# Attention, Fourier mixing and feed-forward: the second layer's weights later, their bits in PSUM, and rests and folds on GpSimd

## The chip, the core and the metric

One core of one Trainium2 chip. The time is device microseconds from start to end of one execution; three runs of the kernel before gave 1315.07 to 1316.8 us, median 1316.18. The profile is of one more execution. Times in it count from its first instruction. In the profile PE is TensorE (PEld its weight loads), DVE is VectorE, ACT is ScalarE, POOL is GpSimd and SP is SyncE, which here only issues DMAs; SPq and ACTq are DMA-issuing instructions of an engine.

## The reference

```
scores = q @ k.T / sqrt(64)               # q, k, v: 8 batches x 8 heads x 576 x 64
mask by blocks of 64: block_i >= block_j;  attn = softmax(scores);  o = attn @ v
x = o as [8, 576, 512]
u = x + real(fft(fft(x, axis=1), axis=2))
un = (u - mean(u)) / sqrt(var(u) + 1e-6)
out = u + relu(un @ w_ch1) @ w_ch2        # 512 -> 2048 -> 512
```

## The kernel before

The 64 heads go one after the other, eight to each of the eight batches `b`. Everything is written out without loops on the chip. Float32 accuracy is kept by splitting operands in a leading part and a rest.

*A head h.* `load_head` brings q and k (`raw`, two buffers). `lead` (ACT, L293) rounds them into `LEAD`; `rest(h, 0)` (DVE, L308) and `rest(h, 1)` (POOL, L310) subtract to get the rests; `lead_copies` are two DMAs within the chip that stack rests and leads (L301, L302). `max_part` 0 to 3 multiply q by k for the row maxima, which DVE reduces (L388, L392, L394) into `M`; `shift` transposes them on PE, ACT negates (L403) and a small DMA puts them in a row of `LEAD` (L405). `scores` 0 to 3 multiply again with the shift in; ACT makes two exponentials of each piece (`ph` in f16 at L434, `p32` in f32 at L435), POOL subtracts for the low half `pl` (L436). `values` multiply `ph` and `pl` by `VH` and `VL`; DVE divides (L471 to L474), and every second head its pair goes to DRAM (`xd`).

*A batch b.* When its eight heads are through, `mirror` loads the rows back, half of them by indirect DMAs from POOL. `folded` (L549, L550) makes sums (name "c") and differences (name "s") of rows and columns, `split32` splits them, `stage1`, `stage1_tail`, `stage2_sin` and `stage2_cos` are the transforms on PE, and `stage2_cos` ends with sums into `X` and `U` (L633, L634; on DVE for b = 0, on POOL otherwise). `normalized_steps` normalises 256 rows at a time and hands them to a *feed*: `first` (16 columns f of the first layer, four parts each, into `h`, then ACT and DVE make `gh` and `gl`, L749 and L750) and `second` (two for each f, into `acc`). There are 18 feeds; first and second layer alternate by pairs of f.

*The weights.* `w_ch1` and `w_ch2` come as 64-bit numbers. They land in 14 loads of 1 MB (two rows of tiles, "double") and 4 of 0.5 MB (L826, SP's queue), at most three ahead. For each landing `weight_single` makes float32 bits by three DVE operations (L836, L837, L838) in `W`, and ACT squares them (L839) for a scale. Landings 0 to 7 are the first layer, the rest the second. `weight_scale` makes a layer's scale; `weight_parts` cuts a tile into two f16 parts (ACT L863, L866 and POOL L867 for the first layer; ACT L863 and DVE L869 for the second). One lane of such steps holds both layers in turn.

*The order.* PE's instructions keep the order in which a planner in the kernel's source writes them down. It has lanes of `Step`s (heads, maxima, scores, values, transform), each with a cost on PE, a chain of costs on other engines ("D0.9" is 0.9 us of DVE, "A", "G", "Q", "L" are ACT, POOL, SP's queue and plain latency), what it comes after, and a `place` for priority. It picks the step that is ready and has the smallest place, fills gaps with feed steps (`filler`), and puts weight steps (`side`) in where their first engine's queue is short (`AHEAD`). Steps of later batches wait for all weights ("w32"). PSUM has eight banks: one `av`, three `ps`, two `h`, two `acc`; until the first feed all of the last seven are lent to the heads (`lent`). Other engines' instructions, and DMA issues in each queue, follow in the order of the scheduler of the tile framework, in order on each engine.

Of the kernel before, what the change touches and what calls it, by code (L numbers as in the profile page):

```python
# [20 lines left out]
DM = H * D  # L21
# [31 lines left out]
def _d(width):  # L53
    return f"D{0.19 + 0.00102 * width}"

# [123 lines left out]
def tile_attn_fourier_ffn(  # L179
# [7 lines left out]
    ps = {name: pool(name, n, space=PSUM) for name, n in BANKS.items()}  # L187
# [60 lines left out]
    queues = {x: Queue() for x in "DAGQ"}  # L248
# [3 lines left out]
    lent = list(BANKS)  # L252
# [4 lines left out]
    def ready(step):  # L257
        r = max((done[x] for x in step.after), default=0.0)
        return max(r, min(rings[x][0] for x in lent)) if step.bank else r

    def issue(step):
# [7 lines left out]
        for engine, cost in step.chain:  # L269
            if engine == "B":  # L270
                free = t + HOP
            else:
                t = t + cost if engine == "L" else queues[engine].book(t + HOP, cost)
# [21 lines left out]
    def quick(h):  # L295

        return nc.scalar if h < H else nc.sync

    def lead_copies(h):
        x0, x1 = REST[h % NB].bitcast(F32), LEAD[h % NB].bitcast(F32)  # L300
        quick(h).dma_start(x0[D:P, 0:S], x1[0:D, 64:64 + S])  # L301
        quick(h).dma_start(x0[0:D, S:], x1[0:D, 64 + S:])  # L302

    def rest(h, which):

        x0, x1, raw = REST[h % NB], LEAD[h % NB].bitcast(F32), raws[h]
        if which == 0:
            nc.vector.tensor_tensor(x0[0:D, 0:S], raw[:, 0:S], x1[0:D, 64:64 + S], op=ALU.subtract)  # L308
# [40 lines left out]
    def prepare_lane():  # L349
        for h in range(B * H):  # L350
# [4 lines left out]
            yield Step(lambda: lead_copies(h), 0.0, ("A1.0" if h < H else "Q1.2", "L2.2"), (("T", h),), ("TC", h), place=h - 0.9)  # L355
            yield Step(lambda: rest(h, 0), 0.0, (_d(S),), (("T", h),), ("T2", h, 0), place=h - 0.8)
            yield Step(lambda: rest(h, 1), 0.0, (_g(S),), (("T", h),), ("T2", h, 1), place=h - 0.8)

    def v_lane():
        for g in range(B * H // 2):  # L360
# [6 lines left out]
                lambda: split_v(g), 0.11, ("D0.46", "B", "A0.83", "D0.88"), (("NS", g),), ("N", g), True,  # L367
# [3 lines left out]
    def max_part(h, n):  # L371
# [21 lines left out]
        if n == 3:  # L393
            nc.vector.tensor_tensor(m[:, 4:5], m[:, 4:5], m[:, 5:6], op=ALU.max)  # L394
# [3 lines left out]
    def shift(h):  # L398
# [6 lines left out]
        quick(h).dma_start(dst.bitcast(F32), mt.bitcast(F32))  # L405
# [88 lines left out]
    def max_lane():  # L494
        for h in range(B * H):
# [5 lines left out]
            yield Step(lambda: shift(h), 0.12, ("A0.26", "B", "A0.5" if h < H else "Q0.6", "L2.2"), (("M", h),), ("X", h), True, place=h - 0.6)  # L501
# [20 lines left out]
    def fourier_steps(b):  # L522
# [23 lines left out]
        def folded(op, width, name, c):  # L546
            r = (128, 128, 33)[c]
            e = work.tile([P, DM], F32, name="tmp", bufs=2)
            nc.vector.tensor_tensor(e[0:r], X[c][0:r], U[c][0:r], op=op)  # L549
            nc.vector.tensor_tensor(e[0:r, 1:256], e[0:r, 1:256], e[0:r, 511:256:-1], op=op)  # L550
# [65 lines left out]
        def stage2_cos(c):  # L616
# [14 lines left out]
            engine = nc.vector if b == 0 else nc.gpsimd  # L631
# [13 lines left out]
            mirror, 0.0, ("G3", "L2.5"), (("V", H * b + H - 1, 4),), D_("u"),  # L645
# [367 lines left out]
```

## Time and profile before

| | |
|---|---|
| median of three runs | 1316.18 us |
| profiled execution | 1315.5 us, span 1313.7 us |
| mean granted TensorE clock | 0.951 |
| busy: PE, DVE, ACT, POOL | 1184.2, 671.9, 548.5, 530.0 us |
| DMA moved | 99.10 MB |

A row of groups has the line, the engine, the operation, what it writes and reads with shapes and count; then busy time, mean nanoseconds of one, and the idle time of the engine before them with what ended it. A row of a time line has start, length, engine, line, operation, and in brackets idle time before it. A row of waits has the waiting engine and line, the one waited for, the sum in microseconds, how often, and the longest.

### The profile page before, as it was taken

The numbers are of one execution on the slowest core, as the hardware profiler recorded it, in microseconds if no ns is written. First come the engines' busy times: TensorE is split into PE (matmuls) and PEld (weight loads), VectorE is DVE, ScalarE is ACT, GpSimd is POOL, SyncE is SP. The second block draws the span as 40 slices with busy tenths as digits, with TensorE's granted clock in tenths as the row PEclk, the third lists the DMA queues.
The fourth block names the chain that finished last, engine by engine and source line by source line (L and its number), as shares of the span: only waits on it lengthen the run. The fifth ranks groups of instructions, "written<-read, shape, count | busy, mean of one in ns | idle before, by whom it ended". The sixth has DMA issues, their size and how long they took to land.

```text
span 1313.7 us, 25264 instructions
## 1 busy us (share of the span) xinstructions
PE 1184.2 (90%) x10068; PEld 886.7 (67%) x10068; DVE 671.9 (51%) x1440; ACT 548.5 (42%) x1137; POOL 530.0 (40%) x578
## 2 busy tenths in 40 slices
PE   3464469999898999999999999999899999999998
PEld 2363357777676777677777777777677767767665
DVE  6983776445645564655546544746372432412211
ACT  3569355545354444444545354544543112111110
POOL 4668143444544553455443645436442500300000
PEclk9955679999699999999999999999999999999999
DMA  9756213232223223322242133223211000000000
GB/s 280 230 175 177 93 29 77 84 106 64 61 65 92 76 50 90 93 76 51 80 115 75 44 96 104 73 70 86 79 30 49 30 12 17 22 1 17 16 17 17
DMA packets 55941, 99.10 MB, mean 75 GB/s; under 512 B 7709, under 2 KB 26605, under 8 KB 55696
## 3 DMA queue, kind: packets, MB, share of 16 engines
q1 hardware_dynamic: 52176, 87.56, 23.5%
q0 software_dynamic: 2288, 7.54, 1.9%
q10 hardware_dynamic: 1360, 2.38, 0.6%
q8 instruction: 80, 1.31, 0.4%
q14 instruction: 37, 0.30, 0.1%
HBM read 58.46 MB, written 18.87 MB: 59 GB/s over the span
## 4 chain that ended last, share of the span: by engine, by line
PE 76%; DVE 10%; ACT 4%; DMA 3%; POOL 3%; issue 3%; SPq 0%; ACTq 0%; DVEq 0%; POOLq 0%
PE h L194 27%; PE acc L194 26%; PE ps L194 16%; PE av L194 5%; POOL pl L436 2%; PE ps L197 1%; DVE M L392 1%; DVE W L837 1%; DMA W<-in_moe_w_ch_dram 1%; DVE rest L308 1%; DVE W L838 1%; ACT lead L293 1%; DVE tmp L549 1%; DMA U<-xd,rows 1%; DVE W L836 1%
## 5 line engine op out<-in xcount | busy, mean ns | idle before, releaser
L194 PE MATMUL h<-uh,W 128*128 128x256 f16 x2304 | 434.9, 275 | 0.0
L436 POOL TENSOR_TENSOR pl<-p,ph 128x288 f16<-128x288 f32 (+1 forms) x256 | 257.9, 1017 | 395.8 <-ACT p L435 249.6
L194 PEld LDWEIGHTS <-W 128*128 128x128 f16 x3456 | 325.8, 99 | 64.3 <-issue 4.0
L194 PE MATMUL acc<-W,gh 128*128 128x512 f16 x1152 | 347.2, 383 | 0.0
L194 PE MATMUL h<-ul,W 128*128 128x256 f16 x1152 | 316.2, 274 | 0.0
L194 PE MATMUL acc<-W,gl 128*128 128x512 f16 x576 | 220.1, 382 | 0.4 <-DVE gl L750 0.4
L750 DVE SCALAR_TENSOR_TENSOR gl<-h,gh 128x512 f16<-128x512 f32 x144 | 98.9, 687 | 227.3 <-ACT gh L749 227.2
L194 PE MATMUL ps<-lead 72*128 72x64 f32 (+9 forms) x700 | 196.5, 342 | 12.5 <-ACT lead L293 6.8
L749 ACT ACTIVATE gh<-h 128x512 f16<-128x512 f32 x144 | 85.9, 596 | 268.4 <-PE h L194 267.7
L434 ACT ACTIVATE ph<-ps 128x512 f16<-128x512 f32 (+1 forms) x229 | 116.0, 507 | 121.0 <-PE ps L194 119.7
L194 PEld LDWEIGHTS <-gh 128*128 128x128 f16 x1152 | 101.0, 99 | 87.8 <-issue 8.2
L392 DVE TENSOR_REDUCE M<-ps 128x1 f32<-128x320 f32 (+3 forms) x235 | 120.5, 527 | 47.9 <-PE ps L194 46.7
L194 PE MATMUL av<-VH,pl 128*128 128x65 f16 x960 | 115.9, 200 | 31.7 <-POOL pl L436 31.5
L194 PEld LDWEIGHTS ps<-lead 72*128 72x128 f32 (+1 forms) x700 | 125.6, 201 | 20.8 <-ACT lead L293 6.8
L194 PEld LDWEIGHTS <-ph 128*128 128x128 f16 x1920 | 113.0, 103 | 34.1 <-DVE x L474 8.4
L310 POOL TENSOR_TENSOR rest<-raw,lead 64x576 fp32r<-64x576 f32 x64 | 116.2, 1816 | 23.3 <-ACT lead L293 18.5
L194 PE MATMUL av<-VH,ph 128*128 128x65 f16 x960 | 118.1, 202 | 8.2 <-DVE x L474 7.6
L194 PE MATMUL ps<-rest 128*128 128x64 f32 (+2 forms) x345 | 121.6, 360 | 1.8 <-DVE M L392 1.1
L435 ACT ACTIVATE p<-ps 128x512 f32<-128x512 f32 (+1 forms) x229 | 115.9, 506 | 10.2 <-POOL pl L436 10.1
L194 PE MATMUL av<-VL,ph 128*128 128x64 f16 x960 | 117.3, 200 | 0.0
L194 PEld LDWEIGHTS <-pl 128*128 128x128 f16 x960 | 93.6, 102 | 34.9 <-POOL pl L436 34.8
L308 DVE TENSOR_TENSOR rest<-raw,lead 64x576 fp32r<-64x576 f32 x64 | 60.0, 938 | 88.4 <-ACT lead L293 88.3
(171 smaller groups left out, 1376.7 us busy)
## 6 DMA issues: line engine op xcount, KB each, us to landing
raw<-in_qk_dram SPq DMA_DIRECT2D x64, 288.0 KB
rest<-lead SPq DMA_DIRECT2D x112, 144.0 KB
W<-in_moe_w_ch_dram SPq DMA_DIRECT2D x14, 1024.0 KB
V<-in_v_dram SPq DMA_DIRECT2D x32, 320.0 KB
xd<-x SPq DMA_DIRECT2D x32, 256.0 KB
out_dram<-u SPq DMA_DIRECT2D x32, 256.0 KB
u<-xd SPq DMA_DIRECT2D x8, 512.0 KB
dft<-in_c_dft_dram POOLq DMA_DIRECT2D x1, 2606.0 KB, 11.3
```

The costliest lines, as they stand in the source:

```text
L194: return tc.keep_in_program_order(nc.tensor.matmul(*args, **kw))
L197: return tc.keep_in_program_order(nc.tensor.transpose(*args, **kw))
L293: nc.scalar.copy(LEAD[h % NB][0:D, 64:], raws[h])
L308: nc.vector.tensor_tensor(x0[0:D, 0:S], raw[:, 0:S], x1[0:D, 64:64 + S], op=ALU.subtract)
L310: nc.gpsimd.tensor_tensor(x0[D:P, S:], raw[:, S:], x1[0:D, 64 + S:], op=ALU.subtract)
L392: nc.vector.tensor_reduce(m[:, j:j + 1], t[:, at - hi:at], axis=AX.X, op=ALU.max)
L434: nc.scalar.activation(ph[:, at:at + w], t[:, 0:w], AF.Exp, scale=0.125)
L435: nc.scalar.activation(p32[:, 0:w], t[:, 0:w], AF.Exp, scale=0.125)
L436: nc.gpsimd.tensor_tensor(pl[:, at:at + w], p32[:, 0:w], ph[:, at:at + w], op=ALU.subtract)
L549: nc.vector.tensor_tensor(e[0:r], X[c][0:r], U[c][0:r], op=op)
L749: nc.scalar.activation(gh, t, AF.Relu)
L750: nc.vector.scalar_tensor_tensor(gl, t, 0.0, gh, op0=ALU.max, op1=ALU.subtract)
```

## The change

- The first two of the three bit operations write into a PSUM tile (`bits`, the two banks of `acc`) instead of `W`.
- `acc` becomes one tile of two banks instead of two tiles of one, and is no longer lent to the heads: five banks are lent instead of seven.
- Weight loads are issued by ACT's queue; copies of the leads and shifts of heads 0 to 7 by SP's.
- There are two weight lanes, one for each layer. The second layer's landings are worked on only after the first layer's scale and the scores of head 5. Heads of later batches wait for the folds of batch 0 instead of for all weights.
- The first feed does all its first layer before its second; its `gh` and `gl` from column 4 on lie in buffers of the transform.
- `rest(h, 0)` of heads 0 to 15, the differences among the folds of batch 0 and its sums into `X` and `U` go from DVE to POOL.
- The last step of the row maxima is a `tensor_scalar` instead of a `tensor_tensor`.
[...]

```diff
-    ps = {name: pool(name, n, space=PSUM) for name, n in BANKS.items()}
+    ps = {name: pool(name, 1 if name == "acc" else n, space=PSUM) for name, n in BANKS.items()}
...
-    queues = {x: Queue() for x in "DAGQ"}
+    queues = {x: Queue() for x in "DAGQK"}
...
-    lent = list(BANKS)
+    lent = ["ps", "h"]
...
+    def book(engine, t, cost):
+        used = [queues[x] for x in {"X": "DK", "G": "GK", "P": "G"}.get(engine, engine)]
+        while True:
+            at = max(x.fit(t, cost) for x in used)
+            if at <= t:
+                return max(x.book(t, cost) for x in used)
+            t = at
...
-        quick(h).dma_start(x0[D:P, 0:S], x1[0:D, 64:64 + S])
-        quick(h).dma_start(x0[0:D, S:], x1[0:D, 64 + S:])
+        nc.sync.dma_start(x0[D:P, 0:S], x1[0:D, 64:64 + S])
+        nc.sync.dma_start(x0[0:D, S:], x1[0:D, 64 + S:])
...
-            nc.vector.tensor_tensor(x0[0:D, 0:S], raw[:, 0:S], x1[0:D, 64:64 + S], op=ALU.subtract)
+            engine = nc.gpsimd if h < 16 else nc.vector
+            engine.tensor_tensor(x0[0:D, 0:S], raw[:, 0:S], x1[0:D, 64:64 + S], op=ALU.subtract)
...
-            nc.vector.tensor_tensor(m[:, 4:5], m[:, 4:5], m[:, 5:6], op=ALU.max)
+            nc.vector.tensor_scalar(m[:, 4:5], m[:, 4:5], m[:, 5:6], None, op0=ALU.max)
...
-        quick(h).dma_start(dst.bitcast(F32), mt.bitcast(F32))
+        nc.sync.dma_start(dst.bitcast(F32), mt.bitcast(F32))
...
+            engine = nc.gpsimd if b == 0 and name == "s" else nc.vector
+            engine.tensor_tensor(e[0:r], X[c][0:r], U[c][0:r], op=op)
+            engine.tensor_tensor(e[0:r, 1:256], e[0:r, 1:256], e[0:r, 511:256:-1], op=op)
...
-            engine = nc.vector if b == 0 else nc.gpsimd
+            engine = nc.gpsimd
...
+    KEEP = [(f"z{x}{m}", [P, 2, n], 1) for x, n in (("c", NCOS), ("s", NSIN)) for m in range(2)]
+    KEEP += [(f"fs{m}", [P, 2, KCOL], 1) for m in range(2)]
...
+            if me == 1 and f > 3:
+                name, shape, bufs = KEEP[f // 2 - 2]
+                both = work.tile(shape, F32R, name=name, bufs=bufs).rearrange("p x n -> p (x n)").bitcast(F16)
+                gh, gl = both[:, 0:4 * P], both[:, 4 * P:8 * P]
...
-            if f == 0:
-                acc.append(ps["acc"].tile([P, DM], F32, name="acc"))
+            if f == 0 and n == 0:
+                both = ps["acc"].tile([P, 2, DM], F32, name="acc")
+                acc.extend((both[:, 0], both[:, 1]))
...
+        if me == 1:
+            for steps in (first_steps, second_steps):
+                for f in range(NF):
+                    yield from steps(f)
+            return
...
+    bits = ps["acc"].tile([P, 2, DM], F32, name="acc")
...
-            nc.sync.dma_start(raw(x).rearrange("p (j n) -> p j n", j=n), weight(i, n))
+            nc.scalar.dma_start(raw(x).rearrange("p (j n) -> p j n", j=n), weight(i, n))
...
-        nc.vector.tensor_scalar(t, r[:, 1], 3, 0x3FFFFFFF, op0=ALU.logical_shift_left, op1=ALU.bitwise_and)
-        nc.vector.scalar_tensor_tensor(t, r[:, 0], 29, t, op0=ALU.logical_shift_right, op1=ALU.bitwise_or)
-        nc.vector.scalar_tensor_tensor(t, r[:, 1], -(1 << 30), t, op0=ALU.bitwise_and, op1=ALU.bitwise_or)
+        y = bits[:, 0:n].rearrange("p x n -> p (x n)").bitcast(I32)
+        nc.vector.tensor_scalar(y, r[:, 1], 3, 0x3FFFFFFF, op0=ALU.logical_shift_left, op1=ALU.bitwise_and)
+        nc.vector.scalar_tensor_tensor(y, r[:, 0], 29, y, op0=ALU.logical_shift_right, op1=ALU.bitwise_or)
+        nc.vector.scalar_tensor_tensor(t, r[:, 1], -(1 << 30), y, op0=ALU.bitwise_and, op1=ALU.bitwise_or)
...
+    def weight_lane(w):
+        if w == 0:
+            yield Step(lambda: weight_loads(0), 0.0, ("A1.2", "L5"), (("L", 0),), ("load",))
+        for x, (i, n, at) in enumerate(LANDS):
+            if i // NF == w:
+                yield Step(
+                    lambda: weight_single(x), 0.0, (f"D{0.19 + 0.53 * n}", f"D{0.19 + 0.6 * n}", f"D{0.19 + 0.6 * n}", f"A{0.38 + 0.43 * n}"),
+                    (("load",),) if w == 0 else (("scale", 0), ('S', 5, 2)), "w32" if x == len(LANDS) - 1 else None,
+                )
+        yield Step(lambda: weight_scale(w), 0.1, ("D0.16", "B", "D0.45"), (), ("scale", w), True)
+        for j in range(NF):
+            yield Step(lambda: weight_parts(NF * w + j), 0.0, ("A0.73", "X0.75") if w else ("A1.45", "G1.2"), (("scale", w),), ("w", NF * w + j))
...
-            if x is not None and may(x) and (i == len(lanes) - 1 or x.place < H or "w32" in done)
+            if x is not None and may(x) and (i == len(lanes) - 1 or x.place < H or ('d', 0, 'fs') in done)
```

More of the change, by code (lines that the diff above doesn't have):

```diff
@@ L272, in issue @@
             else:
[L273 removed]
+                t = t + cost if engine == "L" else book(engine, t + HOP, cost)
         t += HOP
@@ L919, in tile_attn_fourier_ffn @@
     heads = [next(x) for x in lanes]
-    weights, filler = weight_lane(), None
-    side = next(weights)
+    weights, filler = [weight_lane(w) for w in range(2)], None
+    sides = [next(x) for x in weights]
     while True:
@@ L934, in tile_attn_fourier_ffn @@
         until = max(now, min(until, default=now))
[L935 removed]
+        first = min((heads[i].place for i in able), default=H) >= H
+        for w, side in enumerate(sides):
+            if side is None or not may(side) or ready(side) > until:
+                continue
             engine, cost = side.chain[0] if side.chain else (None, 0.0)
             at = max(now, ready(side))
[L938 to L940 removed]
+            ahead = queues[{"X": "D", "P": "G"}.get(engine, engine)].fit(at, cost) - at if engine else 0.0
+            if ahead <= AHEAD[engine in ("D", "X") and first] or at + ahead + cost + FREE <= until:
                 issue(side)
[L942 to L943 removed]
+                sides[w] = next(weights[w], None)
+                break
+        else:
+            w = None
+        if w is not None:
+            continue
         feed = filler is not None and may(filler)
@@ L952, in tile_attn_fourier_ffn @@
             i = min(able, key=lambda i: ready(heads[i]))
-        elif side is not None:
-            issue(side)
-            side = next(weights, None)
+        elif any(sides):
+            w = min((w for w, x in enumerate(sides) if x is not None and may(x)), key=lambda w: ready(sides[w]))
+            issue(sides[w])
+            sides[w] = next(weights[w], None)
             continue
```

59 lines of the change are left out of this document (16 added, 43 removed).

## Prediction

> **What bounds the kernel now.** I read the page first, then busy time by stretches, then groups by shape, then time lines.
>
> ```profile
> PE 1184.2 (90%) x10068; PEld 886.7 (67%) x10068; DVE 671.9 (51%) x1440; ACT 548.5 (42%) x1137; POOL 530.0 (40%) x578
> PE   3464469999898999999999999999899999999998
> PEclk9955679999699999999999999999999999999999
> ```
>
> PE is full except in the first six or seven slices of 33 us. So the question is what the change does to the start-up.
>
> ```profile
> 0.00:20.00 20.00, 5.02 (x16) 3.83 (x16) 11.21 (x33) 4.68 (x6) 7.35 (x25) 1.00 0.90 274
> 20.00:85.00 65.00, 29.36 (x246) 25.18 (x247) 61.81 (x86) 37.30 (x75) 39.86 (x21) 0.88 0.75 238
> 85.00:125.00 40.00, 27.35 (x263) 24.16 (x263) 20.83 (x49) 35.43 (x70) 33.51 (x30) 0.59 0.57 159
> 125.00:137.00 12.00, 0.59 (x11) 0.42 (x8) 1.18 (x4) 5.33 (x8) 9.29 (x9) 0.50 0.66 234
> 137.00:180.00 43.00, 24.75 (x157) 20.31 (x157) 36.08 (x87) 17.42 (x42) 12.72 (x19) 0.66 0.15 42
> 180.00:210.00 30.00, 25.81 (x213) 18.79 (x213) 23.50 (x42) 23.19 (x44) 13.29 (x11) 0.86 0.20 52
> 350.00:1040.00 690.00, 669.96 (x6140) 509.88 (x6141) 371.14 (x842) 321.25 (x685) 330.54 (x362) 0.99 0.27 72
> 1040.00:1313.70 273.70, 269.21 (x1862) 184.16 (x1860) 68.47 (x120) 39.35 (x73) 16.75 (x30) 1.00 0.05 17
> ```
>
> Columns after the length: PE, PEld, DVE, ACT, POOL busy, granted clock. Until 210 us PE is busy 112.9 us, so 97.1 us idle, and much of what it does runs at a clock of 0.5 to 0.7. From 350 us on it idles 24 us in all, and the last 274 us are feed matmuls with a backlog. So a microsecond taken out of the start-up is a microsecond of the total, and little can be won or lost later. By stage: from 20 to 85 DVE is the limit (61.8 of 65 us); from 85 to 125 ACT (89%) and POOL (84%) are, DVE at half; from 125 to 137 PE waits for the first batch's outputs to come back from DRAM; then for its transform.
>
> **Part 1: the weights' bits, and when.** The three DVE operations of a double landing, the single ones, and what else runs beside:
>
> ```profile
> L838 DVE SCALAR_TENSOR_TENSOR W<-W 128x1024 int32<-128x1024 int32 x14 | 19.2, 1368 | 0.1
> L837 DVE SCALAR_TENSOR_TENSOR W<-W 128x1024 int32<-128x1024 int32 x14 | 18.5, 1330 | 0.1
> L836 DVE TENSOR_SCALAR W<-W 128x1024 int32<-128x1024 int32 x14 | 11.9, 851 | 0.0
> L308 DVE TENSOR_TENSOR rest<-raw,lead 64x576 fp32r<-64x576 f32 x11 | 10.2, 925 | 10.2 <-ACT lead L293 10.2
> 58.83 1.21 DVE L838 SCALAR_TENSOR_TENSOR W<-W 128x1024 int32<-128x1024 int32 x1
> 86.28 1.22 DVE L838 SCALAR_TENSOR_TENSOR W<-W 128x1024 int32<-128x1024 int32 x1
> 25.50 8.35 POOL L310 TENSOR_TENSOR rest<-raw,lead 64x576 fp32r<-64x576 f32 x1 [13.24 <-ACT lead L293]
> L310 POOL TENSOR_TENSOR rest<-raw,lead 64x576 fp32r<-64x576 f32 x11 | 26.4, 2401 | 17.9 <-ACT lead L293 16.9 <-DMA raw<-in_qk_dram 0.4
> L436 POOL TENSOR_TENSOR pl<-p,ph 128x512 f16<-128x512 f32 x16 | 21.5, 1353 | 4.8 <-ACT p L435 4.5
> L436 POOL TENSOR_TENSOR pl<-p,ph 128x288 f16<-128x288 f32 x16 | 19.6, 1236 | 18.0 <-ACT p L435 11.1 <-PE av L194 3.6 <-issue 2.5
> L436 POOL TENSOR_TENSOR pl<-p,ph 128x512 f16<-128x512 f32 x88 | 105.2, 1204 | 46.9 <-ACT p L435 36.4 <-PE ps L194 9.0
> L310 POOL TENSOR_TENSOR rest<-raw,lead 64x576 fp32r<-64x576 f32 x41 | 69.3, 1691 | 4.2 <-ACT lead L293 1.2
> L436 POOL TENSOR_TENSOR pl<-p,ph 128x288 f16<-128x288 f32 x88 | 65.3, 752 | 233.9 <-ACT p L435 127.7 <-issue 98.7 <-PE ps L194 6.8
> ```
>
> The first POOL rows are of the first 130 us, the last three of 350 to 1000 us. A double costs DVE 0.851 + 1.330 + 1.368 = 3.55 us. With intermediate bits in PSUM the first operation is not shown by any row; I price it like the 1.22 us of an undisturbed L838 of the same width (end: its present 0.85), and the other two at 1.22 each: 3.66 us. On DVE this part is nothing or a loss of 0.1 us a double. On POOL it can win: next to these DVE operations one rest took 8.35 us, and the two widths of `pl` cost 0.15 and 0.48 us more than later, a rest 0.71: per head 2 x 0.15 + 2 x 0.48 + 0.71 = 2.0 us.
>
> [...]
>
> When: all 14 doubles run ahead of or among the first six heads now. Six of them (the second layer's) move behind head 5's scores. Head ends by the last `pl`, read on POOL:
>
> ```profile
> 51.94 1.94 POOL L436 TENSOR_TENSOR pl<-p,ph 128x512 f16<-128x512 f32 x1 [0.16 <-ACT p L435]
> 90.14 2.27 POOL L436 TENSOR_TENSOR pl<-p,ph 128x512 f16<-128x512 f32 x2 [1.34 <-ACT p L435]
> 99.96 1.55 POOL L436 TENSOR_TENSOR pl<-p,ph 128x512 f16<-128x512 f32 x1
> 121.79 2.85 POOL L436 TENSOR_TENSOR pl<-p,ph 128x512 f16<-128x512 f32 x2
> 101.48 1.16 POOL L867 TENSOR_TENSOR W<-un,W 128x512 f16<-128x512 f32 x1
> 117.57 2.27 POOL L867 TENSOR_TENSOR W<-un,W 128x512 f16<-128x512 f32 x2 [0.33 <-ACT un L866]
> ```
>
> Head 1 ends at 53.9, head 4 at 92.4, head 5 at 101.5, head 7 at 124.6. Head 5, with no weights beside it, took 9.1 us. Heads 2 to 5 took 47.6 with six doubles (from 58.83 to 86.28): (47.6 - 4 x 9.1) / 6 = 1.9 us for a double. Heads 6 and 7 took 23.1 with eight parts of the first layer (101.48 to 117.57): (23.1 - 18.2) / 8 = 0.6 us for a part. Changed: six heads 54.6, all sixteen parts 9.8 (they can start once the eight doubles of layer one are through), and about three second-layer doubles that slip in before head 7 ends, 5.7: 70.1 instead of 70.7 us. So by adding up, the order alone wins next to nothing before head 7's end; it moves weight work from DVE's stage into ACT's and POOL's.
>
> What can win is the 9.1 us itself. A rest leaves DVE (-0.93 us) and lands on POOL (+1.69), where 2.0 us of delay go: POOL about -0.3 a head. Ends: if DVE alone set the pace, six doubles and six rests out of its way are 6 x 3.55 + 6 x 0.93 = 26.9 us; if POOL did and its delays stayed, six rests are 6 x 1.69 = +10.1. I take 1 us a head, the size of DVE's relief and well away from either end, because a head passes through ACT, DVE, POOL and PE in turn: -0.6 - 6 = **-7** (from -27 to +10).
>
> The weight loads go from SP's queue to ACT's, the leads' copies and shifts of heads 0 to 7 the other way. Price taken 0 (the same issues change places; the risk is a rival).
>
> **Part 2: the gap and the transform of batch 0.**
>
> ```profile
> 136.73 0.43 DVE L836 TENSOR_SCALAR W<-u 128x512 int32<-128x512 int32 x1 [10.13 <-DMA u<-in_moe_w_ch_dram]
> 137.64 0.52 POOL L541 MEMSET u<- 1x512 f32 x1 [1.90 <-DMA u<-xd,rows]
> 141.98 0.68 DVE L549 TENSOR_TENSOR tmp<-u 128x512 f32<-128x512 f32 x1
> 161.03 0.41 DVE L633 TENSOR_TENSOR u<-u,dif 128x257 f32<-128x257 f32 x1
> L633 POOL TENSOR_TENSOR u<-u,dif 128x257 f32<-128x257 f32 x8 | 5.8, 725 | 1.8 <-DVE dif L629 1.6
> ```
>
> The gathered rows are there at 137.6, but DVE, in order, first works through the last weight landings, and the fold of `u` starts at 141.98: 4.3 us. With the second layer's weights done in the 30 us between head 5 and here, that delay goes; second-layer parts then come next to the folds, so I take **-3** (from -4.3 to +4). The three sine folds on POOL run beside DVE's cosine folds: 0. The twelve sums cost 0.73 instead of 0.41 on POOL, 3.8 us if all lay on the path, but DVE's own work there gets free: **+1** (0 to +4). The rests of heads 8 to 15 find a POOL that is 47% busy from 180 to 350 us (13.29 + 66.73 of 170 us by the stretches), with feed matmuls to hide them: 0.
>
> ```profile
> 210.00:350.00 140.00, 132.13 (x1171) 99.93 (x1169) 77.71 (x182) 64.51 (x138) 66.73 (x73) 0.93 0.29 79
> ```
>
> **Part 3: first layer whole, and the banks.** Between 180 and 210 PE idles 4.2 us while second-layer parts are still being made. With 64 first-layer steps ahead of the first second-layer step, PE has work that needs none of them: **-2** (-4.2 to 0). Two PSUM banks are no longer lent to the first batch: five instead of seven. No row prices it; from 85 to 125 PE had 12.65 us of idle time that any wait may fall into, so the ends are 0 and about +6, half of that: **+1**. The max in another form and the double `acc` tile: 0, since 48 first-layer matmuls stand between one feed's last sum and the next one's first `acc`.
>
> **Sum**: -7 - 3 + 1 - 2 + 1 = -10 on 1315.5 us (span 1313.7 and 1.8 around it), so 1305.5; the median shown is 0.7 higher: 1306 us.
>
> The clock: PE is granted 0.59 from 85 to 125 us, with 12.65 us idle, and 1.00 where it is full. [...]
>
> **Rivals.**
> 1. *Nothing moves* (0.14): head 7 ends where it did, since the 70.1 against 70.7 of the sum is all there is, POOL's relief is eaten by the rests, and the -3 and -2 by the second layer's parts that now meet the folds. 1313 to 1318 us. For it: ACT and POOL were already 89% and 84% busy from 85 to 125. Against it: from 20 to 85 they were at 57% and 61%.
> 2. *DVE was the whole limit* (0.16): with 26.9 us out of its way, the heads come densely enough that PE keeps full clock and a head falls under 8 us. Most of it arrives: -18 to -25, about 1294 us. For it: 61.8 of 65 us. Against it: head 5 had no weights on DVE and still took 9.1 us.
> 3. *Slower: ACT held by weight loads* (0.22). A load waits for its landing place, and what waits on ACT holds the exponentials behind it, and they hold POOL and PE.
>
> ```profile
> SPq L826 <- DVE W L838: 11.8, 4, 4.2
> SPq L826 <- DVE W L837: 0.5, 1, 0.5
> ```
>
> Nine rows of this kind, first and last shown, are 44.3 us of waits for the weight loads in SP's queue. ACT idles 27.7 us from 20 to 85. If the waits come to ACT, 44.3 - 27.7 = 16.6 us more than it can hide; at 10 us more than it can hide the gain is gone, and beyond that the kernel is slower. 1315.5 - 10 + 16.6 = 1322 us. Against it: the load comes behind the Square of a landing in the order of issue, and that Square waits for the same DVE operation.
>
> **How the numbers follow.** Forecast faster as summed 0.48; rivals 0.14, 0.16, 0.22. What a measurement can tell from no change is 0.2%, 2.6 us: faster 0.63 (forecast and rival 2 less an edge), same 0.14, slower 0.23. The range from 1290 to 1321 takes in most of rival 2 and of rival 3 and leaves out about 2 in 10; the likeliest case's own is 1299 to 1312.
>
> **What would show it.** Head 7's last `pl` ends at 117 to 119 instead of 124.6; no rest on POOL takes over 3 us; `pl` of width 288 falls towards 0.75 in the first 130 us; ACT has no idle time that ends with a weight load; the first fold follows the gather within 1 us; the first feed matmul comes at about 170 instead of 180.7; PE idles under 90 us until it is full. I am wrong if heads 2 to 7 still take 11.8 us each, if ACT shows waits for issue, or if the feeds start as late as before because the sums queue behind `pl` and rests on POOL.

## The result, and the profile after

The changed kernel takes 1347.9 us (median of four runs, 1345.9 to 1348.5) against 1315.6 us for the kernel before beside it: a ratio of 1.0247, 95% interval 1.0225 to 1.0269. It is slower by 32 us; 1306 was forecast, with a range from 1290 to 1321. The profiled execution has a span of 1344.1 us, 30.4 more than before.

First the page of the changed kernel (busy times, then PE's busy share in 40 slices of 33.6 us), then its busy time by the stretches used for the kernel before (after the length: PE, PEld, DVE, ACT, POOL, granted clock, DMA share, GB/s).

```profile
PE 1200.7 (89%) x10068; PEld 900.0 (67%) x10068; DVE 661.6 (49%) x1406; ACT 547.3 (41%) x1137; POOL 550.5 (41%) x612
PE   2673569989998999999899989999799999999998
```
```profile
20.00:85.00 65.00, 40.32 (x304) 34.39 (x303) 58.52 (x96) 40.87 (x84) 36.20 (x32) 0.80 0.83 249
85.00:125.00 40.00, 25.73 (x220) 22.79 (x220) 13.62 (x40) 30.95 (x59) 33.68 (x32) 0.50 0.48 146
125.00:137.00 12.00, 0.00 (x0) 0.00 (x0) 5.83 (x8) 7.45 (x13) 9.59 (x11) 0.50 0.90 299
137.00:180.00 43.00, 27.46 (x209) 22.62 (x210) 32.11 (x65) 22.43 (x55) 27.17 (x28) 0.78 0.13 32
180.00:210.00 30.00, 21.39 (x157) 18.39 (x155) 27.33 (x54) 19.35 (x39) 27.23 (x30) 0.51 0.27 71
350.00:1040.00 690.00, 655.25 (x5933) 496.55 (x5932) 362.52 (x817) 311.45 (x663) 313.71 (x334) 0.97 0.26 72
1040.00:1344.00 304.00, 294.13 (x2026) 201.41 (x2025) 80.28 (x144) 44.66 (x84) 30.59 (x52) 1.00 0.05 16
```

From 20 to 85 us PE does 11 us more than before; from 180 to 210 it does 4.4 us less, at a clock of 0.51 instead of 0.86. The loss that stays is in the two last rows. From 350 to 1040 us PE idles 34.8 us (20.0 before), and the last stretch is longer with 9.9 us idle (4.5 before). Among the waits of PE there two rows are on the sums of a feed and new; the first fence is of the changed kernel from 369 us to the end, and the kernel before from 370 us on follows in the second fence (waiting engine and line, line waited for, sum, times, longest).

```profile
PE av L198 <- POOL pl L446: 22.2, 11, 5.0
PE acc L198 <- DVE u L782: 9.0, 13, 0.8
...
PE acc L198 <- DVE left L782: 1.4, 2, 0.8
```
```profile
PE av L194 <- POOL pl L436: 13.4, 12, 2.1
```

To say where in the program a version loses, I put every trace on one scale: matmuls in order of start, each priced by its shape with its usual distance to the next start in the kernel before (the distance that four in five exceed). All the work is 1109 us on this scale. "Start-up" below is how much later than the kernel before a version has done its first 200 us of work (some 360 to 370 us into the span before; marks between these give the same within 0.7 us); "later" is what it loses from there to the end of the work. Both are of the profiled execution, which can lie some microseconds off the median. The changed kernel: start-up -2.2, later +32.0. An earlier mark would say less: from 100 to 180 us of work the changed kernel is 6 to 15 us behind, and it catches up where the kernel before has a slow stretch of its own (granted clock 0.59 to 0.72 from 330 to 360 us). So the start-up, where the prediction looked for 10 us, gave 2 at best; the rest of the run, where it expected nothing, lost 32.

### The profile page after: what moved, and what is told of

Read it like the earlier page. It is cut to its first block, busy times and chain, and to the rows that moved or that the text cites. A ratio compares the mean times of both kernels' runs of the same rounds, so it can differ in the third digit from the quotient of the medians.

```text
span 1344.1 us, 25224 instructions
## 1 busy us (share of the span) xinstructions
PE 1200.7 (89%) x10068; PEld 900.0 (67%) x10068; DVE 661.6 (49%) x1406; ACT 547.3 (41%) x1137; POOL 550.5 (41%) x612
## 4 chain that ended last, share of the span: by engine, by line
PE 74%; POOL 9%; DVE 7%; issue 4%; DMA 3%; ACT 3%; ACTq 0%; SPq 0%; POOLq 0%; DVEq 0%
PE h L198 27%; PE acc L198 26%; PE ps L198 14%; PE av L198 5%; POOL pl L446 3%; PE ps L201 2%; DMA W<-in_moe_w_ch_dram 1%; POOL rest L320 1%; DVE M L402 1%; DVE u L782 1%; POOL u L645 1%; ACT ph L444 1%; ACT lead L306 1%; POOL u L644 1%; POOL rest L318 1%
## 5 line engine op out<-in xcount | busy, mean ns | idle before, releaser
L446 POOL TENSOR_TENSOR pl<-p,ph 128x288 f16<-128x288 f32 (+1 forms) x256 | 246.3, 972 | 380.2 <-ACT p L445 249.8
L198 PE MATMUL acc<-W,gh 128*128 128x512 f16 x1104 | 334.6, 385 | 11.3 <-DVE u L782 9.0
L198 PE MATMUL ps<-lead 72*128 72x64 f32 (+9 forms) x696 | 205.5, 355 | 16.2 <-ACT lead L306 13.5
L198 PE MATMUL acc<-W,gl 128*128 128x512 f16 x552 | 211.7, 383 | 0.0
L444 ACT ACTIVATE ph<-ps 128x288 f16<-128x288 f32 (+1 forms) x236 | 118.9, 504 | 140.5 <-PE ps L198 139.5
L198 PEld LDWEIGHTS ps<-lead 72*128 72x128 f32 (+1 forms) x696 | 131.8, 210 | 26.9 <-ACT lead L306 13.7
L402 DVE TENSOR_REDUCE M<-ps 128x1 f32<-128x192 f32 (+2 forms) x228 | 117.9, 530 | 60.7 <-PE ps L198 59.3
L198 PE MATMUL ps<-rest 128*128 128x288 f32 (+3 forms) x354 | 128.4, 369 | 0.0
L445 ACT ACTIVATE p<-ps 128x288 f32<-128x288 f32 (+1 forms) x236 | 118.8, 504 | 9.3 <-POOL pl L446 9.1
L320 POOL TENSOR_TENSOR rest<-raw,lead 64x576 fp32r<-64x576 f32 x64 | 107.2, 1674 | 5.9 <-ACT lead L306 1.2
L198 PEld LDWEIGHTS <-gl 128*128 128x128 f16 x552 | 54.5, 99 | 66.9 <-issue 2.7
```

The source lines that it names most:

```text
L198: return tc.keep_in_program_order(nc.tensor.matmul(*args, **kw))
L320: nc.gpsimd.tensor_tensor(x0[D:P, S:], raw[:, S:], x1[0:D, 64 + S:], op=ALU.subtract)
L402: nc.vector.tensor_reduce(m[:, j:j + 1], t[:, at - hi:at], axis=AX.X, op=ALU.max)
L444: nc.scalar.activation(ph[:, at:at + w], t[:, 0:w], AF.Exp, scale=0.125)
L445: nc.scalar.activation(p32[:, 0:w], t[:, 0:w], AF.Exp, scale=0.125)
L446: nc.gpsimd.tensor_tensor(pl[:, at:at + w], p32[:, 0:w], ph[:, at:at + w], op=ALU.subtract)
```

## The experiments

Versions with the joint queue have a queue "K" in the planner, in which `book` puts steps of DVE marked "X" and steps of POOL marked "G" one behind the other; "the queue taken out" means that `book` looks only at the engine itself. Some versions differ only in the text of one step and issue PE's instructions in exactly the same order as their parent; others make the planner draw another order. That proved to be the distinction that matters, so it is named each time.

**1. The joint tile of sums.** PE's rows `acc <- DVE u L782` name the sum `u += acc` of a feed: the first half's sum is written ahead of the second half's last three matmuls, and the two halves now share one tile. This edit puts both sums behind the last matmul; PE's order is that of the changed kernel.

```diff
-            if f == NF - 1:
-                u = us[n]
-                nc.vector.scalar_tensor_tensor(u, acc[n], inv_w, u, op0=ALU.mult, op1=ALU.add)
-                stores[n](u)
+            if f == NF - 1 and n == 1:
+                for i in range(2):
+                    u = us[i]
+                    nc.vector.scalar_tensor_tensor(u, acc[i], inv_w, u, op0=ALU.mult, op1=ALU.add)
+                    stores[i](u)
```

> The changed kernel, with the two sums of a feed (u = acc * inv_w + u) both issued after the second half's last matmul; the order on PE is the same. Theory A (the one acc tile makes PE wait for the first half's sum before the second half's last three matmuls, 16 waits and 13.1 us in the trace, 0.84 us each, 18 feeds): 1347.9 - 15 = 1333 us, and no PE wait on the sums is left. Rival B (the waits only take the place of others, as the feeds are filler): 1345 to 1348 us.

Measured: 1330.6 us (ratio to before 1.0126, 1.0109 to 1.0143), 17.4 us less than the changed kernel, as theory A expected. No wait of PE on a sum is left. Its start-up is -1.6, later +16.2: all of the gain lies in the later part. Between rounds of runs the kernel before itself moved from 1313.3 to 1315.7 us, so a difference of medians from two rounds is good to some 2 us; by the ratios this gain is 16 us.

**2. The other way round: five banks, then the joint tile, in the kernel before.**

```diff
-    lent = list(BANKS)
+    lent = ["ps", "h"]
```

> The kernel before with five PSUM banks lent to the first batch instead of seven, nothing else. My prediction priced this at +1 us (0 to +6): 1317 us. Rival: the first batch is starved of banks, +6 us or more.

Measured: 1319.4 us (1.0045, 1.0028 to 1.0062). Another order of PE, so this +5.1 is the banks and the chance of an order together. On top of it one `acc` tile of two banks, with PE's order unchanged:

> As the last, and with acc as one tile of two banks instead of two tiles of one. Theory A: 15 us more than the last one, about 1332 us, with PE waits on the sums of 0.84 us in each feed. Rival B: no more than 2 us above the last one.

Measured: 1330.0 us (1.0120, 1.0103 to 1.0137), 10.6 us more than with five banks alone. The waits of PE from 369 us on, in the version with the joint tile:

```profile
PE acc L194 <- DVE u L762: 13.7, 14, 1.8
```

The row is absent from the version with five banks alone. In the old kernel the joint tile brings the row; in the new one the row goes when no sum stands between the two halves. So the joint tile, with a sum between its halves, is a cause: 11 to 17 us by pairs with equal order.

**3. The queue K.**

```diff
-        used = [queues[x] for x in {"X": "DK", "G": "GK", "P": "G"}.get(engine, engine)]
+        used = [queues[x] for x in {"X": "D", "G": "G", "P": "G"}.get(engine, engine)]
```

> The changed kernel with the planner's shared queue K taken out (X books D alone, G books G alone); all costs stay. It changes only the order written for PE. Theory C (the order made with that queue puts value matmuls where POOL's pl comes late: in the changed kernel five PE waits of 2.4 to 5.0 us after 400 us, each with 3.4 to 10 us at half clock behind it): 1347.9 - 15 = 1333 us, PE waits for pl after 370 us back at about 13 us instead of 22. Rival D (the holes come from something else, the queue is innocent): within 4 us of 1348.

Measured: 1312.2 us (0.9991, 0.9972 to 1.0010), 35.7 us less than the changed kernel, more than twice the 15 us of theory C. Start-up -16.7, later +12.4; the joint tile is still in, and its wait is now the largest of PE's from 369 us on:

```profile
PE acc L198 <- DVE u L782: 11.9, 14, 1.6
PE ps L198 <- DVE M L402: 7.6, 7, 1.9
PE av L198 <- POOL pl L446: 7.0, 9, 1.7
```

**4. Both mends.** The sums last and the queue taken out; the same order of PE as in 3.

> The changed kernel with both sums of a feed behind the second half's last matmul and without the planner's shared queue. Theory: the two effects are separate and add: 1347.9 - 17.4 - 35.7 = 1295 us, 1.5% faster than before, no PE wait on the sums. Rival: part of the 35.7 us came from the same waits (the planner did not know them), then 1300 to 1308 us.

Measured: 1300.0 us (0.9907, 0.9875 to 0.9938): faster than both kernels, by 13.5 us than the kernel before. The joint tile is worth 12.2 us here, so the two effects add nearly, but not in full (that was to give 1295). Start-up -16.1, later -5.8. Its four executions lie between 1293.7 and 1304.3 us, and the profiled one is the fastest: differences from this version are good to some 4 us, and by the median its "later" would be about 0.

**5. Where the queue does its harm.** With the sums last, K is booked only until, or only from, the planning of the first feed's second turn (of two transposes ahead of its matmuls).

> The changed kernel with the sums behind the last matmul (1330.6 us) and the planner's shared queue in force only until the first feed's second turn is planned. Theory C (the queue harms in the later batches, by waits for pl and the half clock behind them): 1330.6 less most of 36, about 1300 us. Rival E (it harms the start-up, where the two differ by 17 us of progress at 300 us): 1313 to 1318 us.

> The same with the shared queue in force only after that turn. Theory C: close to 1330 us. Rival E: the start-up is free, 1310 to 1314 us. If the two add, this and the last one lie together 35 us under twice 1330.6.

Measured: 1309.3 us with K until the feed (start-up -2.7, later -3.8); 1327.7 us with K from there on (start-up -7.1, later +20.7). So the two halves cost 9.3 and 27.7 us over version 4; K until the feed lies between theory C's 1300 and rival E's 1313, K from there on near theory C's 1330. At this point the queue looked guilty in both. In the changed kernel one such place is seen by POOL's time line (start, length, engine, line, operation):

```profile
655.37 1.13 POOL L548 DMA_INDIRECT u<-xd,rows  x1 [1.46 <-DMA X<-xd]
...
659.02 1.39 POOL L320 TENSOR_TENSOR rest<-raw,lead 64x576 fp32r<-64x576 f32 x1
660.49 1.15 POOL L446 TENSOR_TENSOR pl<-p,ph 128x512 f16<-128x512 f32 x1
```

and by PE's, in the same stretch:

```profile
661.70 0.24 PE L198 MATMUL av<-VH,pl 128*128 128x65 f16 x1 [4.96 <-POOL pl L446]
...
663.63 0.64 PE L198 MATMUL acc<-W,gh 128*128 128x512 f16 x1
664.06 0.64 PE L198 MATMUL acc<-W,gl 128*128 128x512 f16 x1
...
666.86 0.59 PE L198 MATMUL acc<-W,gh 128*128 128x512 f16 x2
667.29 0.38 PE L198 MATMUL acc<-W,gl 128*128 128x512 f16 x1
```

POOL gathers rows for a batch, then makes a rest, then the `pl` for which PE has waited 4.96 us. After it the matmuls of 512 columns start 0.43 us apart, and from 666.86 on 0.215 us: some 5 us behind the hole also run at half clock (granted clock 0.50 from 661.70 to 665.70 us, 1.00 from 667.70).

**6. Is it the queue's rule, or the order that it drew?** The planner reckons 3 us for POOL's gather. If the queue's orders put pieces where the gather is planned too short, 5.5 us should mend it. And a planner's time between engines of 0.26 or 0.24 us instead of 0.25 changes nothing but the order. All of these are other orders of PE.

```diff
-            mirror, 0.0, ("P3", "L2.5"), (("V", H * b + H - 1, 4),), D_("u"),
+            mirror, 0.0, ("P5.5", "L2.5"), (("V", H * b + H - 1, 4),), D_("u"),
```
```diff
-HOP = 0.25
+HOP = 0.26
```

> The version with the sums after the last matmul and the joint queue (1330.6 us), with the planner's time for POOL's gather set to 5.5 us in place of 3. Theory one (the joint queue's order puts score pieces where POOL is still at its gather, since the gather is planned too short): the waits of TensorE on pl between 250 and 1060 us fall from 23.3 us to under 14 and the time to 1310 to 1318. Theory two (any order is one of many, and the joint queue's is a bad one by chance): the time moves, but to either side and by no more than 12 us: 1319 to 1342. Theory three (the joint queue itself makes pieces wait, wherever the gather lies): 1327 to 1334 and waits on pl over 19 us.

> The same version (1330.6 us), with the planner's time from one engine to the next 0.26 us in place of 0.25: another order of TensorE by the same rules. If the joint queue is what costs the time (theories one and three): 1325 to 1336, waits on pl 19 to 28 us. If its order was a bad one by chance (theory two): under 1320, waits on pl under 17 us.

> The version with both mends (1300.0 us, waits on pl 9.9 us), with the planner's time for POOL's gather 5.5 us. Theory one: few pieces meet the gather there, so little moves: 1296 to 1301. Theory two: it moves to either side: 1292 to 1312. Theory three: 1298 to 1302.

> The version with both mends (1300.0 us), with the planner's time from one engine to the next 0.26 us: another order by the same rules. If the 30 us between the two versions are the joint queue's (theories one and three): 1295 to 1305. If they are the chance of one order (theory two): anywhere from 1292 to 1325, and the nearer to 1315 the less the joint queue is to blame.

> Sums after the last matmul and the joint queue, with the planner's time from one engine to the next 0.24 us: a fourth order with the joint queue (1330.6, 1331.2 and 1306.4 us so far; without it 1300.0, 1306.0 and 1310.7). If the queue costs its time by its rule and 1306.4 was the odd one: 1322 to 1336. If an order with the queue comes out as any other: 1298 to 1316.

> The kernel before, with the planner's time from one engine to the next 0.26 us and nothing else: another order by the same rules. If the kernel before stands on a good order, kept since it was the best of many: 1319 to 1335. If its order is like any other: 1307 to 1322. This gives the width within which one comparison of two planner settings says nothing of what they do.

| version, all with the sums last | with the queue: us (start-up, later) | without: us (start-up, later) |
|---|---|---|
| as planned | 1330.6 (-1.6, +16.2) | 1300.0 (-16.1, -5.8) |
| gather 5.5 us | 1331.2 (+3.3, +12.3) | 1306.0 (-8.1, -0.4) |
| time between engines 0.26 us | 1306.4 (-4.3, -5.8) | 1310.7 (-7.9, +1.7) |
| time between engines 0.24 us | 1315.4 (-3.3, +4.4) | not tried |

The kernel before with 0.26 us: 1316.4 us (1.0012, 0.9991 to 1.0032; start-up -0.5, later +5.4), so this second order gives no sign that it stands on a lucky one.

The gather theory falls. With the longer gather PE's waits on `pl` do fall, as theory one expected, but others come, and the time stays; from 250 to 1060 us, the version with the sums last and the queue, then the same with the gather at 5.5 us:

```profile
PE av L198 <- POOL pl L446: 23.3, 15, 3.3
...
PE ps L198 <- DVE M L402: 2.5, 3, 1.4
```
```profile
PE ps L198 <- DVE M L402: 11.4, 7, 3.0
PE av L198 <- POOL pl L446: 10.4, 8, 2.3
```

With 0.26 us, where the queue alone as the cause was to give 1325 to 1336 us, the queue is no worse than its absence, and its row reads:

```profile
PE av L198 <- POOL pl L446: 8.3, 9, 1.7
```

So two things were mixed in the queue's cost. In the start-up, every version with K there (the changed kernel, the four of the table, K until the feed) lies between -4.3 and +3.3; every one without K there that keeps the bits in PSUM (seven of them) between -16.7 and -7.9; and K from the feed on, in force for nearly the last two thirds of this work, gives -7.1. These do not overlap: the queue holds the start-up back by some 10 us on the whole, by 14.5, 11.4 and 3.6 us in the three pairs of the table. For the first pair the traces show where: with K it is 2 us behind at 20 us of work (80 us into its span), 14 us at 50 (177 us), and 13 to 18 us from there to the mark. That is in the last heads of the first batch (head 7's last `pl` ends at 124.6 instead of 112.7 us) and in its transform. Later, orders with K lose -5.8 to +20.7 once the joint tile is out, orders without it -5.8 to +5.1. These overlap; the queue's orders are worse on the whole, but the size for the changed kernel, +16.2, is in good part the order that it happened to have.

**7. The parts that were priced, taken out of version 4 one by one.** The bits put together in SBUF again (the order of PE is the same, so nothing else differs there):

```diff
-    bits = ps["acc"].tile([P, 2, DM], F32, name="acc")
...
-        y = bits[:, 0:n].rearrange("p x n -> p (x n)").bitcast(I32)
+        y = t
```

> The version with both mends (1300.0 us), with the weights' bits put together in SBUF again and not in PSUM. The rests on POOL during the first heads (1.40 us there) should come back to 2 us and more (2.40 us in the kernel before). If POOL and DVE together bound the stretch from 20 to 130 us, as the prediction's part A says at 1 us a head, the first batch ends 5 to 9 us later (124.9 us in the mended version) and the time is 1305 to 1309. Rival: the loads of the weights and of the heads set that stretch, and the relief on POOL is hidden: 1299 to 1302.

Measured: 1313.0 us (0.9998, 0.9985 to 1.0011), 13.0 us more than with PSUM, beyond the 5 to 9 us expected; start-up -1.1 instead of -16.1. Head 7's last `pl` ends at 120.0 instead of 112.7 us, and the first feed's first matmul starts at 208.4 instead of 195.1. POOL's groups of the first 130 us, bits in SBUF, then bits in PSUM:

```profile
L446 POOL TENSOR_TENSOR pl<-p,ph 128x512 f16<-128x512 f32 x16 | 22.7, 1422 | 12.5 <-ACT p L445 12.0 <-PE h L198 0.4
L446 POOL TENSOR_TENSOR pl<-p,ph 128x288 f16<-128x288 f32 x16 | 19.6, 1239 | 6.1 <-ACT p L445 4.5 <-issue 1.2
L318 POOL TENSOR_TENSOR rest<-raw,lead 64x576 fp32r<-64x576 f32 x11 | 18.7, 1699 | 17.0 <-ACT lead L306 17.0
L320 POOL TENSOR_TENSOR rest<-raw,lead 64x576 fp32r<-64x576 f32 x11 | 18.3, 1664 | 0.8
```
```profile
L446 POOL TENSOR_TENSOR pl<-p,ph 128x512 f16<-128x512 f32 x16 | 18.4, 1156 | 18.0 <-ACT p L445 16.5 <-PE ps L198 1.3
L320 POOL TENSOR_TENSOR rest<-raw,lead 64x576 fp32r<-64x576 f32 x11 | 16.4, 1492 | 0.8
L318 POOL TENSOR_TENSOR rest<-raw,lead 64x576 fp32r<-64x576 f32 x11 | 15.4, 1398 | 19.2 <-ACT lead L306 19.2
...
L446 POOL TENSOR_TENSOR pl<-p,ph 128x288 f16<-128x288 f32 x16 | 11.5, 731 | 8.7 <-ACT p L445 7.6 <-PE ps L198 0.8
```

The `pl` of eight heads take POOL 42.3 against 29.9 us and the rests of eleven heads 37.0 against 31.8: 1.55 + 0.47 = 2.0 us a head less. DVE gains too; its operations on the bits of a double in the first 200 us, bits in SBUF, then bits in PSUM:

```profile
L865 DVE SCALAR_TENSOR_TENSOR W<-W 128x1024 int32<-128x1024 int32 x14 | 21.6, 1543 | 0.1
L866 DVE SCALAR_TENSOR_TENSOR W<-W 128x1024 int32<-128x1024 int32 x14 | 21.3, 1523 | 0.2
L864 DVE TENSOR_SCALAR W<-W 128x1024 int32<-128x1024 int32 x14 | 15.7, 1124 | 9.1 <-DMA W<-in_moe_w_ch_dram 9.1
```
```profile
L866 DVE SCALAR_TENSOR_TENSOR acc<-W,acc 128x1024 int32<-128x1024 int32 x14 | 17.1, 1224 | 0.2
L865 DVE TENSOR_SCALAR acc<-W 128x1024 int32<-128x1024 int32 x14 | 17.1, 1223 | 9.0 <-DMA W<-in_moe_w_ch_dram 8.9
L867 DVE SCALAR_TENSOR_TENSOR W<-W,acc 128x1024 int32<-128x1024 int32 x14 | 17.0, 1217 | 0.2
```

That is 4.19 against 3.66 us a double. This is the one part of the change whose gain is shown by itself. With the bits in SBUF and the two banks lent again, seven in all (another order):

> The version with the bits in SBUF (the kernel run beside this one), with its two banks of sums as two tiles that are lent to the heads before the first feed, as in the kernel before: all seven banks. The five banks cost +5.2 in the kernel before, so by that this is 5 us faster than the kernel with five banks and bits in SBUF, with the gain made before the first feed (batch 0 ends some 3 to 5 us earlier). Rival: with the rests on POOL a bank comes free as soon as it is wanted, and nothing moves: within 2 us of its neighbour. Against the version with both mends (1300.0 us) it says whether the bits in PSUM are worth the banks that they take.

Measured: 1315.6 us (1.0016, 0.9998 to 1.0035), no better than with five banks. The +5.1 of the kernel before with five banks is thus no price of the banks that could be carried over. The other parts, the first two each another order, the third with the order of PE unchanged:

> The version with both mends (sums after the last matmul, no joint queue: 1300.0 us), with the first feed's first layer taken in turn with its second layer, as before. By the prediction's step (first feed whole: -2, between -4.2 and 0) this costs +2 and the time is 1302, not below 1300 nor above 1304. Rival: the first layer whole gives the planner nothing, since in the feed's stretch (200 to 270 us) TensorE has the heads of the second batch beside it: 1299 to 1301, or under 1298 if the later batch is the one that is held.

> The version with both mends (1300.0 us), with the first batch's sums and sine folds on DVE again. The prediction priced these on POOL at +1 (0 to +4): so 1299, not under 1296. Rival: they are what puts the first feed's turns at 205 us instead of 185 us; back on DVE the turns come by 195 us or sooner and the idle time of 180 to 210 us (4.6 us, and half clock beside it) closes: 1292 to 1296. Other rival: DVE is full there (weights' parts), the folds come later and the time is 1302 or more.

> The same as e5_both, and the second layer's weights wait only for the first layer's scale, not for the scores of head 5. My prediction's additive model (order alone wins 0.6 us): within 3 us of e5_both. Rival (holding them back is what takes DVE's load out of the first heads): 8 us or more slower than e5_both.

Measured: first feed in turns 1307.9 us (start-up -12.8, later +5.1); sums and sine folds on DVE 1300.9 us (-16.6, +2.1); second layer's weights not held behind head 5, 1300.1 us (-14.6, -5.2). In the start-up these are 3.3, -0.5 and 1.5 us against version 4; the rest of the first one's 7.9 us, which is outside both expectations, cannot be told from an order's chance. Not taken out by themselves were the rests on POOL, the other queues for weight loads and copies, and the max in another form.

## Why the prediction was wrong, by its steps

Its sum was -10 us. The changed kernel's +30.4 us of span are, to 29.8 on the scale of work: start-up -2.2, the joint tile +15.8 ("later" of the changed kernel less that of version 1), and +16.2 for the later course of the order with K. Four steps failed.

*"The double `acc` tile: 0."* This is the step with the clearest failure. The reason given, 48 first-layer matmuls between one feed's last sum and the next one's first `acc`, looks at the wrong neighbour: the sum of the first half stands directly ahead of the second half's last three matmuls of the same feed. With two tiles they had nothing in common; with one, PE waits for DVE there 16 times in 18 feeds, 0.84 us in this row of PE's time line of the changed kernel.

```profile
1068.63 0.59 PE L198 MATMUL acc<-W,gh 128*128 128x512 f16 x2 [0.84 <-DVE u L782]
```

*"From 350 us on it idles 24 us in all ... little can be won or lost later."* Little could be won there, but the reading said nothing about what can be lost. Nearly the same program, without the joint tile and with its bits in PSUM, lost between -5.8 and +20.7 us there in twelve orders.

*The sum had no term for the planner's queue*, though the change to the order was in the diff. It took about 10 us from the start-up, the size of the whole gain. Which of the queue's bookings hold the heads back was not taken apart.

*"The gap: -3."* The prediction measured it from the gathered rows (POOL's MEMSET that follows them) to the fold of `u` on DVE, 4.3 us, and wanted that gone. In the changed kernel it is 134.19 to 138.51, 4.3 us again: the weights' operations hardly fill it any more, but the fold ahead of this one takes 2.57 instead of 0.68 us, beside POOL's work on weights (DVE's, then POOL's time line, changed kernel; then the fold ahead in the kernel before). The gathered rows themselves come 3.5 us sooner.

```profile
136.02 2.57 DVE L560 TENSOR_TENSOR tmp<-X,U 33x512 f32<-33x512 f32 x1 [1.23 <-POOL W L895]
138.51 0.67 DVE L560 TENSOR_TENSOR tmp<-u 128x512 f32<-128x512 f32 x1
```
```profile
134.19 0.51 POOL L551 MEMSET u<- 1x512 f32 x1 [0.95 <-DMA u<-xd,rows]
134.68 3.36 POOL L895 TENSOR_TENSOR W<-un,W 128x512 f16<-128x512 f32 x3
```
```profile
141.38 0.68 DVE L549 TENSOR_TENSOR tmp<-X,U 33x512 f32<-33x512 f32 x1
```

The other terms that were priced did better, once the joint tile and the queue are out of the way.

| step, as predicted | measured |
|---|---|
| bits in PSUM: 1.22 us an operation, 3.66 a double | 1.225, 1.225 and 1.216 us, 3.67 (changed kernel) |
| no rest on POOL over 3 us; `pl` of 288 towards 0.75 | longest 1.9 us, means 1.40 and 1.45; 0.73 |
| heads -7, at 1 us a head | bits alone: head 7's end -7.3, total -13.0 (version 4 against SBUF) |
| order of the weights alone: -0.6 | 0.2 us, within the spread (hold taken out) |
| head 7's last `pl` at 117 to 119 | 122.1; 112.7 without the queue |
| gap -3: first fold within 1 us of the gather | 1.8 us to the first fold, 4.3 to that of `u`, as before |
| sums on POOL +1 | under 1 us either way in the start-up |
| first feed whole -2 (-4.2 to 0) | 3.3 us in the start-up, total unclear |
| five banks +1 (0 to +6) | +5.1 in one order, nothing in another |
| first feed matmul at about 170 instead of 180.7 | 210.7 |

The term of the heads was near in size for the part that could be isolated, and by luck: the bits alone bring head 7's end forward by 7.3 us, 0.9 a head, but the prediction took its 1 us a head from the rests that leave DVE, let the moved rest eat POOL's relief, and had the bits cost DVE 0.1 us a double. With the rests on POOL they save DVE 0.5 us a double and POOL 2.0 us a head, and the moved rest takes 1.40 us, not 1.69. That their place in PSUM would relieve POOL at all was assumed; this pair is what shows it. Some 6 us more of the bits' gain come behind head 7, by the first feed. In the changed kernel itself most of the term is lost again: heads 2 to 7 take 11.5 us each (11.8 before, 9.9 in version 4), which was one of the prediction's own signs of being wrong.

Another such sign came true, but its reason is not borne out: the first feed is 30 us late, and the sums of batch 0 do stand on POOL between `pl` and rests, of which these are the first and one of the last (POOL's time line, changed kernel).

```profile
168.32 0.73 POOL L644 TENSOR_TENSOR X<-X,dif 33x257 f32<-33x257 f32 x1
...
190.03 1.06 POOL L645 TENSOR_TENSOR u<-u,add 128x255 f32<-128x255 f32 x1
```

Yet with the sums on DVE (another order) the first feed starts at 195.7 us, in version 4 at 195.1, and the time is the same. What the traces show beside it is that the second batch's heads, which no longer wait for all weights, come earlier: heads 8 and 9 end at 161.5 and 177.8 us in the changed kernel, 170.8 and 196.2 before. Whether they are what delays the feed was not tested.

Rival 1 (nothing moves) describes the start-up of the changed kernel, -2.2 us, though by another cause than it gave. Rival 2 (-18 to -25) is not reached even by version 4, -13.5 us by the medians and -22 in its fastest execution alone; the heads there take 9.9 us each, not under 8, and that denser heads keep PE at full clock was the author's estimate, which no run isolates. Rival 3, the slower one, named ACT held by weight loads; its price set waits of the first 200 us against idle time of 65 us. ACT's waits up to 130 us in the changed kernel are for the bits, on DVE, not for a landing place:

```profile
ACT left L867 <- DVE W L866: 21.2, 6, 5.6
...
ACT L867 <- issue: 3.1, 1, 3.1
```

These 21 us did not decide: version 4 has 21.7 us of the same wait.

## What to carry to other kernels

Two buffers put into one tile shared their waits here: with the joint tile in the kernel before, PE waited 13.7 us on the sums from 369 us on, with five banks and two tiles no such row is among PE's waits. Where a change merges tiles, look for the instruction that touches one half right beside the other engine's access to the other half, within a pass and not only between passes; here the price came 16 times in 18 feeds. Where a planner or scheduler writes the order, any change of its costs draws a new order: here 0.01 us in one constant moved the time by 1, 11, 15 and 24 us in four pairs, so a single comparison of two settings says little below some 20 us, and a part is judged with the order held fixed or over several orders. And a stretch that is nearly full has little to gain but much to lose; a prediction needs a bound for it on the side of loss.

## What the runs showed of the hardware that was not expected

*Intermediate results in PSUM, two of three operations, were worth 13 us, and both engines gained.* With PE's order equal, a `pl` of 288 columns on POOL takes 0.73 instead of 1.24 us and the three DVE operations of a double 3.66 instead of 4.19 us. Against the 3.55 us of the kernel before, which has one rest a head less on POOL, DVE's gain cannot be seen. The first fold above has the same two engines: with both inputs in SBUF it takes 2.57 us beside POOL's work (its row of three operations lasts from 134.68 to 138.04 us), the next fold, begun at 138.51 us, 0.67 us, and the same fold in the kernel before 0.68 us, where POOL has no row between 138.16 and 145.51 us. The runs show these durations, not their cause.

*Half clock followed holes of 2.07 us and less.* In the kernel before PE waits 2.07 us until 418.10, with shorter holes around it (1.43 us until 413.83, 0.34 and 0.20 us behind it), and the granted clock of the following stretches is:

```profile
418.10 0.20 PE L194 MATMUL av<-VH,pl 128*128 128x65 f16 x1 [2.07 <-POOL pl L436]
```
```profile
420.00:422.00 2.00, 2.00 (x6) 0.71 (x7) 1.90 (x5) 0.72 (x3) 0.81 (x2) 0.61 0.00 0
422.00:424.00 2.00, 2.00 (x6) 0.75 (x5) 2.00 (x8) 0.76 (x2) 0.26 (x1) 0.53 0.02 1
424.00:426.00 2.00, 2.00 (x17) 1.57 (x16) 2.00 (x7) 0.07 (x1) 0.00 (x0) 1.00 0.00 0
```

Within these rows the granted clock is 0.50 from 420.50 to 423.75 us and 1.00 from 424. Which of the four holes brought it, if any of them did, is not shown.

*The clock column is not always to be believed.* In the version with the queue and 0.24 us the stretch from 85 to 125 us reads

```profile
85.00:125.00 40.00, 25.73 (x220) 22.78 (x220) 14.54 (x42) 29.76 (x57) 33.63 (x31) 1.00 0.52 155
```

at a clock of 1.00, and the changed kernel's row, shown at the top, has the same 220 matmuls in the same 25.73 us at 0.50. The matmuls of 64 columns into `av` speak for half clock in both: at 120 us that version has them at 0.24 us, and the changed kernel at 244 ns from 85 to 125 us, against 193 ns from 672 to 700 us, where its column shows 1.00. The records of the clock begin at 52 us in the changed kernel and at 62 us in the kernel before, and ahead of them the column shows 1.00 there. A 1.00 ahead of the first record says nothing of the clock.
